# Block 0's tokens split a layer earlier, the first long unit begun inside the last output, and fetches, stores and splits of the second network reordered

## The chip, the cores and the metric

One core of one Trainium2 chip runs the whole program. The metric is the device time of one execution in microseconds; runs of this kernel are compared by their median. The profile comes from one execution of its own.

## The reference

Three layers follow each other: windowed attention (4 batches, 8 heads, 576 positions, head size 64, half of the heads with a dilated window), a gated network and a second network. x is the attention's output, 2304 tokens of 512 values.

```python
x = attention(q, k, v)                     # (2304, 512)
gate = 1.0 / (1.0 + np.exp(-(x @ w_gate)))     # 512 -> 1536
x = (gate * (x @ w_val)) @ w_out               # 1536 -> 512
h = x @ w_in                                   # 512 -> 2048
g = np.maximum(h, 0.0) + alpha * np.minimum(h, 0.0)
return g @ w_out2                              # 2048 -> 512
```

Everything is fp32 in and out. The kernel writes each operand as a high and a low fp16 half, scaled by powers of two, and makes each product from three matmuls (high x high, high x low, low x high).

## The kernel before

**Stages.** The program is one list of instructions for each engine, in the order in which the Python code issues them; nothing is reordered afterwards. A batch b has twelve steps m, in which `gv_mm` makes the gate's and the value's product into pairs of PSUM banks (three pairs in turn, `buffer`), ACT takes the sigmoid (L597), DVE multiplies (L602) and `gv_halves` makes the fp16 halves `gt` (L612 on ACT, the subtraction L170 on POOL or DVE). After that come four outputs d of the first network, each twelve groups `o1_mm(b, d, m)` of six matmuls of 288 columns (L636), evacuated by `o1_y` (L654), which stores y to DRAM (L656). I call the twelve steps layer 1 of the batch and the four outputs its layer 2. Between them `prepare` takes entries of a list of steps that make the second network's weights (w_in2 into `wi_dram`, w_out2 into `w2_dram`: L813 to L816 on POOL, L823 on ACT, L828 on DVE, stores L840 on SP). Batch 3 is the last; `last_output(d, m)` puts further work into its layer 2.

**The second network** works in token blocks: block 0 has 256 tokens, blocks 1 to 4 have 512. `y_load` fetches a block's y, `y_sums` makes differences on POOL, and ACT and DVE split them (`y_high` L925, `y_low` L929, or in steps, `y_steps` L914 and L915) into the tile `yh`. Block 0 is multiplied directly in four short units of two products each, which are issued at fixed points of outputs 2 and 3. Blocks 1 to 4 have four long units each, which use Strassen's scheme in Winograd's form: seven products P1 to P7 of twelve matmuls (L968, 256 columns) instead of eight. In a long unit the products pile up in banks: x takes P1, then P6, P5 and P3 on top; y takes P2; z takes P7, then P4. Since P1 alone is wanted too, ACT copies the bank x away (`copy`, L1023) ahead of each next product, and DVE adds the copies elsewhere (`plus`, L1026): c1 to P2, c4 and z for a22, c2 to z. `relu` (L1006) and `slopes` (L1014) make the activation, `g_high` (L1050) and `g_low` (L1054) its halves.

**Filling.** Behind each of a unit's seven products `spare()` takes items of the output product `out2_mm` (L1213) of the block before: three matmuls an item for block 0, six for the others, 56 items a block, spread evenly over the 28 slots of a block. `out2_done` evacuates a finished product on ACT or DVE (L1236, L1238) and issues its store (L1243).

**SP's queue** issues all DMAs in program order; an issue that waits holds up all behind it. `in2_fetch` (L761) brings the weights of a unit (two tiles of 896 KB; four tiles in a ring, two used, two ahead), `w2_fetch` (L1196) those of an output product (two of 512 KB; four places). Both are issued at the end of a unit, behind the stores that its items issued.

**Buffers.** The pool `yp` has 8 slots of 4 KB a partition, which all loads of words, quarters, halves and y share: a new tile waits until its slot's last reader, often a store, is done. The pool `tp` has two slots for each of the tags `sg` and `gf`.

The lines that set the place of block 0's splits, of the fetches, and of P1:

```python
            if d < 2 and m == 0:                       # last_output
                y_load(d)
            if d == 1 and m in (6, 8):
                y_high(0, m // 8)
                y_low(0, m // 8)
...
                unit(j, k, spare, n if n[0] < NJ else None)
                in2_release()
                while coming and ring_i:
                    in2_fetch(coming.popleft())
                w2_fetch_all()
```

## Time and profile before

| | us |
|---|---|
| runs shown | 857.73, 858.0, 858.41 |
| median | 858.0 |
| profiled execution | 857.94 |
| its span, first to last instruction | 856.1 |
| TensorE busy | 826.2 |
| VectorE busy | 601.8 |
| ScalarE busy | 438.4 |
| GpSimd busy | 263.8 |

The span is 1.84 us shorter than the profiled execution. Batch 3's layer 1 runs from 398 to 469.6 us, its layer 2 with the short units from 469.6 to 533.0, block 1 from 533.0 to about 589, blocks 2 to 4 and the last output product after that. A row of the time order gives the start, the duration, the engine, the line and the tiles, a count where alike instructions follow each other, and in brackets how long the engine had been idle and which instruction ended that. The printed end of a matmul group lies 0.16 us behind the start of the next where nothing waits.

### The profile page before, as it was taken

What the parts mean: (1) busy time and instruction counts of PE and PEld (TensorE: products, weight loads), DVE (VectorE), ACT (ScalarE), POOL (GpSimd) and SP (SyncE); (2) the same over time, 40 slices, a digit from 0 to 9 for tenths busy, and PEclk for the clock granted to TensorE, in tenths of its full rate; (3) what the DMA queues carried; (4) which work ended last, traced back from release to release, by engine and by line L of the source; (5) the groups of instructions that cost most, each with busy time, mean ns of one, the idle gap of its engine ahead of it and who ended that gap; (6) DMA issues with size and microseconds to landing.
All of it is one profiled execution on the core that took longest, in us unless ns stands there. A gap on an engine that the chain in (4) does not pass through costs nothing.

```text
span 856.1 us, 21080 instructions
## 1 busy us (share of the span) xinstructions
PE 826.2 (97%) x8994; PEld 686.5 (80%) x8994; DVE 601.8 (70%) x1046; ACT 438.4 (51%) x725; POOL 263.8 (31%) x253
## 2 busy tenths in 40 slices
PE   7699999999999999999999899998999999999998
PEld 4677787877877778777887678887888888888887
DVE  5889976776687677777859767588577577566641
ACT  4767664357435453444336556465555555454420
POOL 1324252234011011020238744343442245232220
PEclk9699999999999999999999999999999999999999
DMA  9954526334454252068667867955955655675372
GB/s 319 348 184 141 191 73 218 112 121 161 149 190 154 76 202 70 1 201 251 232 218 240 286 242 284 337 204 201 340 206 202 245 183 202 239 284 198 123 230 78
DMA packets 86621, 169.86 MB, mean 198 GB/s; under 512 B 5504, under 2 KB 57856, under 8 KB 86528
## 3 DMA queue, kind: packets, MB, share of 16 engines
q1 hardware_dynamic: 86528, 168.52, 56.8%
q8 instruction: 70, 1.15, 0.6%
q14 instruction: 23, 0.19, 0.1%
HBM read 138.72 MB, written 29.79 MB: 197 GB/s over the span
## 4 chain that ended last, share of the span: by engine, by line
PE 72%; DVE 12%; DMA 9%; ACT 3%; issue 2%; SPq 2%; POOL 0%; ACTq 0%; DVEq 0%
PE banks L584 20%; PE banks L1213 18%; PE banks L968 17%; PE banks L636 13%; DMA w_dram<-halves 2%; DVE plain L189 2%; DMA plain_dram<-plain 2%; DVE plain L185 2%; PE banks L317 2%; PE banks L431 1%; DVE halves L828 1%; DMA vc<-vk 1%; DMA q<-qbd 1%; DVE plain L181 1%; DVE gf L602 1%
## 5 line engine op out<-in xcount | busy, mean ns | idle before, releaser
L584 PE MATMUL banks<-xh,w_gv 128*128 128x288 f16 x2304 | 290.6, 287 | 0.5 <-ACT sg L597 0.3
L584 PEld LDWEIGHTS <-w_gv 128*128 128x128 f16 x2304 | 223.3, 98 | 58.4 <-issue 0.9
L968 PE MATMUL banks<-yh,w_i 128*128 128x256 f16 x1536 | 189.1, 274 | 10.0 <-ACT yh L925 2.5
L968 PEld LDWEIGHTS <-w_i 128*128 128x128 f16 x1536 | 150.6, 98 | 30.3 <-issue 8.0
L636 PE MATMUL banks<-gt,w_o 128*128 128x288 f16 x1152 | 144.5, 286 | 0.9 <-POOL gt L170 0.9
L636 PEld LDWEIGHTS <-w_o 128*128 128x128 f16 x1152 | 111.8, 98 | 28.9 <-issue 1.1
L1213 PEld LDWEIGHTS <-g_gv 128*128 128x128 f16 x780 | 76.3, 98 | 8.8
L1213 PE MATMUL banks<-w,g_gv 128*128 128x256 f16 x612 | 75.5, 273 | 0.0
L1006 ACT ACTIVATE neg<-banks 128x512 f32<-128x512 f32 x72 | 42.8, 594 | 56.9 <-DVE banks L1026 40.3
L1064 POOL TENSOR_TENSOR yh<-temp_y 128x512 f32<-128x512 f32 x16 | 26.5, 1659 | 125.6 <-DVE temp_y L1014 120.8
L166 POOL TENSOR_SCALAR sc<-sc 128x1 f32<-128x1 f32 x35 | 11.7, 334 | 173.0 <-DVE sc L162 172.9
L1213 PEld LDWEIGHTS <-g_g 128*128 128x128 f16 x564 | 55.2, 98 | 6.4
L602 DVE SCALAR_TENSOR_TENSOR gf<-banks,sg 128x576 f32<-128x576 f32 x48 | 36.0, 752 | 34.4 <-PE banks L584 25.5
L597 ACT ACTIVATE sg<-banks,sc 128x576 f32<-128x576 f32 x48 | 35.3, 734 | 39.9 <-PE banks L584 30.1
L196 ACT ACTIVATE junk<-plain 128x1024 bf16<-128x1024 f32 x32 | 33.8, 1057 | 36.0 <-DVE plain L200 18.8
L170 POOL TENSOR_TENSOR gt<-gf,gt 128x576 f16<-128x576 f32 x19 | 27.7, 1457 | 75.4 <-ACT gt L612 75.2
L612 ACT ACTIVATE gt<-gf 128x576 f16<-128x576 f32 x48 | 32.4, 677 | 33.3 <-DVE gf L602 29.4
L189 DVE SCALAR_TENSOR_TENSOR plain<-words,plain 128x512 uint32<-128x512 uint32 x64 | 47.7, 765 | 1.2
L1213 PE MATMUL banks<-w,g_g 128*128 128x256 f16 x396 | 48.3, 273 | 0.0
L1054 DVE SCALAR_TENSOR_TENSOR g_gv<-temp_w,sc,g_gv 128x256 f16<-128x256 f32 (+1 forms) x37 | 26.0, 711 | 28.4 <-ACT g_gv L1050 28.4
L1023 ACT ACTIVATE temp_y<-banks 128x512 f32<-128x512 f32 x32 | 19.0, 595 | 50.9 <-PE banks L968 50.7
L185 DVE SCALAR_TENSOR_TENSOR plain<-words,plain 128x512 uint32<-128x512 uint32 x64 | 43.8, 704 | 1.2
(178 smaller groups left out, 1212.3 us busy)
## 6 DMA issues: line engine op xcount, KB each, us to landing
w_i<-wi_dram SPq DMA_DIRECT2D x40, 896.0 KB, 6.3
w<-w_dram SPq DMA_DIRECT2D x52, 512.0 KB, 8.7
words<-w_out SPq DMA_DIRECT2D x28, 512.0 KB, 5.5
plain<-w_dram SPq DMA_DIRECT2D x18, 512.0 KB, 9.5
words<-w_in SPq DMA_DIRECT2D x16, 512.0 KB, 5.2
w_dram<-halves SPq DMA_DIRECT2D x28, 256.0 KB, 5.1
q<-qbd SPq DMA_DIRECT2D x6, 1152.0 KB, 7.6
words<-w_gate SPq DMA_DIRECT2D x12, 512.0 KB, 5.3
```

Source lines behind the costliest of these rows:

```text
L170: engine.tensor_tensor(out=lo, in0=src, in1=hi, op=ALU.subtract)
L185: nc.vector.scalar_tensor_tensor(out=d, in0=hi, scalar=0xC0000000, in1=d, op0=ALU.bitwise_and, op1=ALU.bitwise_or)
L189: nc.vector.scalar_tensor_tensor(out=d, in0=lo, scalar=29, in1=d, op0=ALU.logical_shift_right, op1=ALU.bitwise_or)
L196: nc.scalar.activation(junk[:, :src.shape[1]], src, AF.Square, accum_out=dst)
L584: nc.tensor.matmul(ps[:, h, :], lhsT=a, rhs=x_[:, H2 * h:H2 * h + H2], start=(kk == 0 and i == 0), stop=(kk == KD - 1 and i == 2),)
L597: nc.scalar.activation(halves(sg), ps, AF.Sigmoid, scale=sgx[b][:, m:m + 1])
L602: nc.vector.scalar_tensor_tensor(out=halves(gf), in0=ps, scalar=2.0 ** -15, in1=halves(sg), op0=ALU.mult, op1=ALU.mult)
L612: nc.scalar.activation(t[:, 0, :], gf, AF.Copy)
L636: nc.tensor.matmul(ps[:, h, :], lhsT=a, rhs=x_[:, H2 * h:H2 * h + H2], start=(m == 0 and z == 0), stop=(m == M1 - 1 and z == 2),)
L968: nc.tensor.matmul(o, lhsT=h, rhs=l, start=(new and v == 0 and q == 1), stop=(q == total_), skip_group_check=True,)
L1006: nc.scalar.activation(t[:, :2 * n], src[:, :2 * n], AF.Relu, scale=-1.0)
L1213: nc.tensor.matmul(ps[:, H4 * t:H4 * t + H4].rearrange("p (c f) -> p c f", c=2), lhsT=a, rhs=x_, start=(first and k == 0 and t == 0 and z ...
```

## The change

- Block 0's y is loaded at step m = 4 of batch 3's layer 1, into one yp slot; its differences are made at m = 6 and its splits at m = 7 and 8. `y_first` takes the first `xh` tile for them. The blocks' places in `yh` change sides (even and odd).
- `gv_halves` of the last step stands directly behind its multiply, with the subtraction on DVE, for every batch.
- `o1_y` of batch 3 uses the tag `gf` instead of `sg`.
- `unit_begin(1, 0)` (P1 and its copy) stands at step (3, 9) of layer 2. The copy goes from bank x into a bank y, and P2 is added on top of it; `plus c1` goes. y has two banks in turn (7 and 3), the output products have three instead of four.
- y of block 2 is loaded at (3, 4); its splits, and those of blocks 3 and 4, are spread over the slots of the block before.
- `in2_fetch` stands directly behind P4, `w2_fetch` behind the last item of a product, `out2_store_old` issues a store three items after its evacuation. The first w2 fetch moves from (3, 0) to (3, 8).
- Six items of block 1's own first output product are taken within block 1.

```diff
@@ o1_y
-        dst = tp.tile([P, S], F32, tag="sg", name="y")
+        dst = tp.tile([P, S], F32, tag="gf" if b == B - 1 else "sg", name="y")
@@ y_load, y_first, y_sums
+        if j == DIRECT:
+            t = yp.tile([P, 2, 2, n], F32, tag="y", name="y")
+            for d in range(2):
+                y[j, d] = t[:, d]
+                nc.sync.dma_start(out=t[:, d], in_=y_dram[:, d::2, t0:t0 + n])
+            return
...
+    def y_first():
+        n = blocks[DIRECT][1]
+        t = spans[0] = xp.tile([P, 4608], F16, tag="xh", name="yh")
+        z = 6 * n
+        yh[DIRECT] = [t[:, z * i:z * i + z].rearrange("p (d i t) -> p d i t", d=2, i=3) for i in range(2)]
+        temps["s2"] = t[:, 3584:].bitcast(F32)
...
         if j == DIRECT:
-            add(out=s[:, 0, :n], in0=t[:, 1, :n], in1=t[:, 0, :n], op=ALU.subtract)
+            s = y[j, d, "sums"] = temps["s2"][:, n * d:n * d + n].unsqueeze(1)
+            add(out=s[:, 0], in0=t[:, 1], in1=t[:, 0], op=ALU.subtract)
             return
@@ in2_bank
-            turn["h"] = (turn["h"] + (x_ != "y")) % 3
-            i = in2_order[3 if x_ == "y" else turn["h"]]
+            if x_ == "y1":
+                turn["y"] = 1 - turn.get("y", 0)
+                i = (in2_order[3], 3)[turn["y"]]
+            else:
+                turn["h"] = (turn["h"] + 1) % 3
+                i = in2_order[turn["h"]]
@@ unit_begin, unit
-        copy("c1", in2_mm(j, "x1", [(PART_A[1], PART_B[1])], True, w))
+        in2_mm(j, "x1", [(PART_A[1], PART_B[1])], True, w)
+        in2_bank("y1")
+        nc.scalar.activation(in2_banks["y1"], in2_banks["x1"], AF.Copy)
...
-        ps_y = mm(2, "y", True)
+        ps_y = mm(2, "y")
         rest(0)
-        plus(ps_y, "c1", ps_y)
...
-        ps_z = plus(ps_z, "c2", mm(4, "z"))
+        ps_z = mm(4, "z")
+        in2_release()
+        while coming and ring_i:
+            in2_fetch(coming.popleft())
+        plus(ps_z, "c2", ps_z)
@@ out2_mm, out2_done
-            turn["o"] = (turn.get("o", -1) + 1) % 4
+            turn["o"] = (turn.get("o", -1) + 1) % 3
...
             ring.append(w2q[i].popleft())
+            while ring and fetched:
+                w2_fetch(fetched.popleft())
...
-            nc.sync.dma_start(
+            stores.append([3 if len(items) > U else 0, lambda: nc.sync.dma_start(
...
+            out2_store_old()
@@ last_output
-            if d < 2 and m == 0:
-                y_load(d)
+            if (d, m) == (1, 0):
+                y_load(1)
...
-            if d == 1 and m in (6, 8):
-                y_high(0, m // 8)
-                y_low(0, m // 8)
...
+            if (d, m) == (3, 4):
+                y_load(2)
...
+            if (d, m) == (3, 8):
                 w2_ring(True)
                 w2_fetch(fetched.popleft())
+            if (d, m) == (3, 9):
+                short_order.clear()
+                turn.update(h=-1, y=1)
+                i = 2 * turn["m"]
+                in2_order.extend([6, 4, 5, 7] if i == 4 else [6, 5, 4, 7])
+                unit_begin(1, 0, [w_i[0], w_i[1]])
@@ batch loop
+                if m == M1 - 1:
+                    gv_halves(b, m, False)
...
+                if late and m == 4:
+                    y_first()
+                    y_load(DIRECT)
+                if late and m == 6:
+                    y_sums(DIRECT, 0)
+                    y_sums(DIRECT, 1)
+                if late and m in (7, 8):
+                    y_high(DIRECT, m - 7)
+                    y_low(DIRECT, m - 7)
-            gv_halves(b, M1 - 1, late)
@@ blocks 1 to 4
+            early = U - 2 if j == 1 else 0
+            items.extend((j, 1, k) for k in range(early))
...
-                if more and k in (1, 2):
-                    y_sums(j + 1, k - 1)
-                    background.extend([lambda: None] * 2 + y_steps(j + 1, k - 1))
+                    background.extend([lambda: None] * (7 * (U // 2)))
+                    first = 2 if j == 1 else 7
+                    background[first] = lambda j=j: y_sums(j + 1, 0)
+                    for d in range(2):
+                        for n, f in enumerate(y_steps(j + 1, d)):
+                            background[first + 2 + 9 * d + 3 * n] = f
+                    background[first + 9] = lambda j=j: y_sums(j + 1, 1)
```

The next rows show how this moves instructions. A name with a number is a tile, `banks_81` stands for all of PSUM, and line numbers of the changed kernel differ from those of the profile: its L946 is L929 before, L1131 is the new copy, L1044 is L1023, L1071 is L1050, L1222 is L1196, L1271 is L1243.

DVE between the multiplies of m = 8 and m = 9 in batch 3's layer 1 (halves and quarters are tiles of the w2 steps), before and then after:

```order
L602 SCALAR_TENSOR_TENSOR gf_6833<-banks_81,sg_6774 128x576
L828 SCALAR_TENSOR_TENSOR halves_6804<-quarter_6662,sc_78,halves_6804 128x512
L828 SCALAR_TENSOR_TENSOR halves_6804<-plain_6789,sc_78,halves_6804 128x512
L828 SCALAR_TENSOR_TENSOR halves_6835<-plain_6789,sc_78,halves_6835 128x512
L828 SCALAR_TENSOR_TENSOR halves_6835<-quarter_6659,sc_78,halves_6835 128x512
L828 SCALAR_TENSOR_TENSOR halves_6871<-plain_6790,sc_78,halves_6871 128x512
L602 SCALAR_TENSOR_TENSOR gf_6919<-banks_81,sg_6869 128x576
```

```order
L602 SCALAR_TENSOR_TENSOR gf_6843<-banks_81,sg_6784 128x576
L828 SCALAR_TENSOR_TENSOR halves_6814<-quarter_6666,sc_78,halves_6814 128x512
L828 SCALAR_TENSOR_TENSOR halves_6814<-plain_6799,sc_78,halves_6814 128x512
L946 SCALAR_TENSOR_TENSOR yh_6562<-y_6563,sc_78,yh_6562 128x512
L946 SCALAR_TENSOR_TENSOR yh_6562<-yh_6562,sc_78 128x256
L828 SCALAR_TENSOR_TENSOR halves_6845<-plain_6799,sc_78,halves_6845 128x512
L828 SCALAR_TENSOR_TENSOR halves_6845<-quarter_6663,sc_78,halves_6845 128x512
L828 SCALAR_TENSOR_TENSOR halves_6885<-plain_6800,sc_78,halves_6885 128x512
L602 SCALAR_TENSOR_TENSOR gf_6933<-banks_81,sg_6883 128x576
```

Two split instructions of block 0 now stand among the five w2 instructions; before, they stood behind all of them in layer 2.

ACT at the end of layer 2 (`y_7781` and `y_7795` are the last output, `neg` the activations, the copies come from banks), before and then after:

```order
L1050 ACTIVATE g_gv_7208<-temp_w_7206,sc_78 128x256 x3
L654 ACTIVATE y_7781<-banks_81,sc_78 128x576
L196 ACTIVATE junk_7783,sc_78<-y_7781 128x576
L1050 ACTIVATE g_gv_7208<-yh_7203,sc_78 128x256
L1050 ACTIVATE g_gv_7208<-temp_w_7206,sc_78 128x256
L1050 ACTIVATE g_gv_7208<-yh_7204,sc_78 128x256
L1050 ACTIVATE g_gv_7208<-temp_w_7206,sc_78 128x256
L1023 ACTIVATE yh_7205<-banks_81 128x512
L1023 ACTIVATE temp_y_7812<-banks_81 128x512
```

```order
L1071 ACTIVATE g_gv_7217<-temp_w_7215,sc_78 128x256 x3
L1131 ACTIVATE banks_81<-banks_81 128x512
L654 ACTIVATE y_7795<-banks_81,sc_78 128x576
L196 ACTIVATE junk_7797,sc_78<-y_7795 128x576
L1071 ACTIVATE g_gv_7217<-yh_7213,sc_78 128x256
L1071 ACTIVATE g_gv_7217<-temp_w_7215,sc_78 128x256
L1071 ACTIVATE g_gv_7217<-yh_6562,sc_78 128x256
L1071 ACTIVATE g_gv_7217<-temp_w_7215,sc_78 128x256
L1044 ACTIVATE temp_y_7826<-banks_81 128x512
```

The copy of P1 stood behind the output's evacuation and four `g_high`; now it stands ahead of them.

SP in block 1 (`out` is a store, `w_i` a unit's weights, `w_2` and `plain` places of w2), before and then after:

```order
L1243 DMA out<-temp_7808 128x256
L761 DMA w_i0_6622<-wi_dram_87 128x3584
L761 DMA w_i1_6623<-wi_dram_87 128x3584
L1196 DMA w_2_7813<-w2_dram_89 128x2048 x2
L1196 DMA plain_7589<-w2_dram_89 128x2048
L1196 DMA plain_7590<-w2_dram_89 128x2048
L1243 DMA out<-temp_y_7810 128x256
L1243 DMA out<-temp_7809 128x256
L761 DMA w_i2_6624<-wi_dram_87 128x3584
```

```order
L1222 DMA plain_7755<-w2_dram_89 128x2048
L1271 DMA out<-temp_7822 128x256
L761 DMA w_i0_6626<-wi_dram_87 128x3584
L761 DMA w_i1_6627<-wi_dram_87 128x3584
L1222 DMA w_2_7827<-w2_dram_89 128x2048 x2
L1271 DMA out<-temp_y_7824 128x256
L1222 DMA w_2_7827<-w2_dram_89 128x2048 x2
L1271 DMA out<-temp_7823 128x256
L761 DMA w_i2_6628<-wi_dram_87 128x3584
L761 DMA w_i3_6629<-wi_dram_87 128x3584
```

The w2 fetches stand between the stores, and a store stands three items behind the evacuation that it waits for.

## Rows read from the trace of the kernel before

**Rows 1.** The page's head and part 1: busy us, share, instructions.
```profile
span 856.1 us, 21080 instructions
...
PE 826.2 (97%) x8994; PEld 686.5 (80%) x8994; DVE 601.8 (70%) x1046; ACT 438.4 (51%) x725; POOL 263.8 (31%) x253
```

**Rows 2.** Busy us by stretch: length, PE, PEld, DVE, ACT, POOL, PEclk, DMA share, GB/s.
```profile
600.00:620.00 20.00, 20.00 (x186) 17.92 (x184) 11.20 (x19) 10.06 (x17) 9.41 (x9) 1.00 0.93 352
```

**Rows 3.** TensorE in order of time: start, us, line, tiles, count, idle before.
```profile
469.61 8.49 PE L636 MATMUL banks<-gt,w_o 128*128 128x288 f16 x68
478.97 10.21 PE L636 MATMUL banks<-gt,w_o 128*128 128x288 f16 x82 [0.87 <-POOL gt L170]
491.72 0.27 PE L968 MATMUL banks<-yh,w_i 128*128 128x256 f16 x1 [2.54 <-ACT yh L925]
492.56 0.49 PE L968 MATMUL banks<-yh,w_i 128*128 128x256 f16 x3 [0.57 <-DVE yh L929]
494.09 3.86 PE L968 MATMUL banks<-yh,w_i 128*128 128x256 f16 x20 [1.04 <-DVE yh L929]
...
499.99 2.78 PE L968 MATMUL banks<-yh,w_i 128*128 128x256 f16 x24
...
533.03 2.78 PE L968 MATMUL banks<-yh,w_i 128*128 128x256 f16 x24
536.97 2.78 PE L968 MATMUL banks<-yh,w_i 128*128 128x256 f16 x24 [1.15 <-ACT yh L1023]
...
574.53 1.47 PE L968 MATMUL banks<-yh,w_i 128*128 128x256 f16 x12 [1.03 <-ACT temp_y L1023]
...
577.29 1.47 PE L968 MATMUL banks<-yh,w_i 128*128 128x256 f16 x12 [0.63 <-DVE banks L1026]
...
580.16 1.48 PE L968 MATMUL banks<-yh,w_i 128*128 128x256 f16 x12 [0.75 <-DVE temp_y L1014]
...
589.17 0.83 PE L968 MATMUL banks<-yh,w_i 128*128 128x256 f16 x6 [0.97 <-DMA w_i<-wi_dram]
591.35 0.83 PE L968 MATMUL banks<-yh,w_i 128*128 128x256 f16 x6 [1.36 <-DMA w_i<-wi_dram]
```

**Rows 4.** Busy time by stretch at the second place, columns as before.
```profile
494.00:496.00 2.00, 1.91 (x10) 1.35 (x10) 0.52 (x2) 1.43 (x4) 1.12 (x2) 0.50 1.04 372
496.00:498.00 2.00, 2.00 (x14) 1.55 (x13) 0.00 (x0) 0.00 (x0) 2.00 (x4) 0.69 1.09 384
```

**Rows 5.** SP, ACT and POOL in order of time ahead of the first short unit.
```profile
474.94 3.84 SPq L870 DMA_DIRECT2D y<-y_dram  x2
...
484.75 1.99 ACT L823 ACTIVATE halves<-quarter,sc 128x512 f16<-128x512 f32 x3 [3.86 <-DMA w_dram<-halves]
...
489.59 0.84 POOL L902 TENSOR_TENSOR ys<-y 128x256 f32<-128x256 f32 x1 [4.20 <-DMA w_dram<-halves]
```

**Rows 6.** SP's queue at the end of block 1.
```profile
583.17 0.34 SPq L1243 DMA_DIRECT2D out<-temp  x1
583.61 0.87 SPq L761 DMA_DIRECT2D w_i<-wi_dram  x2
```

**Rows 7.** VectorE: line L828 (min/median/max ns), and the multiply of m = 10.
```profile
L828 DVE SCALAR_TENSOR_TENSOR halves<-quarter,sc,halves x16: 737/1085/1759, 450.5 to 489.1; 128x512 f16<-128x512 f32 x16
...
467.32 0.74 DVE L602 SCALAR_TENSOR_TENSOR gf<-banks,sg 128x576 f32<-128x576 f32 x1
```

**Rows 8.** Line L1023 and line L1026 (min/median/max ns), and the first copy of P1.
```profile
L1023 ACT ACTIVATE temp_y<-banks x32: 574/597/598, 538.5 to 807.8; 128x512 f32<-128x512 f32 x32
...
L1026 DVE TENSOR_TENSOR banks<-banks,temp_y x32: 684/692/700, 542.8 to 814.7; 128x512 f32<-128x512 f32 x32
...
536.34 0.57 ACT L1023 ACTIVATE yh<-banks 128x512 f32<-128x512 f32 x1
```

**Rows 9.** SP's first issue for long units; DMA of 520 to 556 us.
```profile
522.14 7.73 SPq L761 DMA_DIRECT2D w_i<-wi_dram  x4
...
DMA packets 3002, 11.96 MB, mean 332 GB/s; under 512 B 297, under 2 KB 297, under 8 KB 2999
```

More of the change, by code (lines that the diff above doesn't have):

```diff
@@ L1116, in unit @@
             unit_begin(j, k, w)
-        in2_banks["x"] = in2_banks.pop("x1")
+        in2_banks.update((x_, in2_banks.pop(x_ + "1")) for x_ in "xy")
         def mm(i, x_, new=False):
@@ L1242, in out2_done, with out2_store_old @@
             r0 = blocks[j][0] + P * nt * to[0]
-            nc.sync.dma_start(
+            stores.append([3 if len(items) > U else 0, lambda: nc.sync.dma_start(
                 out=out[r0:r0 + P * nt, H4 * to[1]:H4 * to[1] + H4].rearrange("(t p) c -> p t c", p=P),
                 in_=dst.rearrange("p (t c) -> p t c", c=H4),
-            )
+            )])
+            out2_store_old()
+    stores = deque()
+    items = deque()
+    def out2_store_old():
+        while stores and stores[0][0] <= 0:
+            stores.popleft()[1]()
     engines = (nc.gpsimd, nc.vector)
@@ L1417, in take @@
         def take(items):
+            for x_ in stores:
+                x_[0] -= 1
+            out2_store_old()
             j, i, k = items.popleft()
             out2_mm(j, i, k)
-            if k == U - 1 and j == NJ - 1:
-                w2_fetch_all()
         def w2_fetch_all():
@@ L1515, in attention_moe_kernel @@
         second_places()
-        short_order.clear()
-        turn["h"] = 0
-        i = 2 * turn["m"]
-        in2_order.extend([6, 4, 5, 7] if i == 4 else [4, 5, 6, 7])
         w2_ring(False)
-        items = deque((DIRECT, i, k) for i in ORDER for k in range(U))
+        items.extend((DIRECT, i, k) for i in ORDER for k in range(U))
         slots = [7 * (U // 2)]
@@ L1540, in spare @@
                 for _ in range(-(-len(items) // slots[0])):
-                    take(items)
+                    if (items[0][0], items[0][1], items[0][2] // 2) in g2:
+                        take(items)
             slots[0] -= 1
@@ L1551, in attention_moe_kernel @@
                 if more and k == 0:
-                    y_load(j + 1)
-                if more and k in (1, 2):
+                    if j > 1:
+                        y_load(j + 1)
                     assert not background
-                    y_sums(j + 1, k - 1)
-                    background.extend([lambda: None] * 2 + y_steps(j + 1, k - 1))
+                    background.extend([lambda: None] * (7 * (U // 2)))
[5 more added lines that the diff above has]
+                    background[first + 9] = lambda j=j: y_sums(j + 1, 1)
                 n = (j, k + 1) if k + 1 < U // 2 else (j + 1, 0)
                 unit(j, k, spare, n if n[0] < NJ else None)
-                in2_release()
-                while coming and ring_i:
-                    in2_fetch(coming.popleft())
-                w2_fetch_all()
             assert not items, len(items)
-            items.extend((j, i, k) for i in ORDER for k in range(U))
+            items.extend((j, i, k) for i in ORDER for k in range(early if i == 1 else 0, U))
         flush()
```

16 lines of the change are left out of this document (7 added, 9 removed).

## Prediction

> **What bounds the kernel now.** I read the page's head first, then busy time in stretches, then TensorE's own timeline with its waits, then the engines that it waits for. TensorE is busy 826.2 of 856.1 us [rows 1], and from 600 to 840 us, in twelve stretches of 20 us alike, it is busy throughout [rows 2]. The change neither adds nor removes a matmul, so it can only win back idle time of TensorE, and only between 460 and 600 us; what else it touches (the last halves of batches 1 and 2, the long units after 600) has no idle time behind it. The reader should see ten idle times there [rows 3], in five places:
>
> - 0.87 us in the last output of batch 3 (478.97), behind the low half of the last `gt` on POOL.
> - 2.54 + 0.57 + 1.04 = 4.15 us before the first short unit (491.72 to 494.09), behind the splits of block 0's tokens, L925 on ACT and L929 on DVE.
> - 1.15 us in the first long unit (536.97): P6 waits for ACT's copy of P1 out of the bank that P6 adds to.
> - 1.03 + 0.63 + 0.75 = 2.41 us in block 1 (574.53 to 580.16), behind ACT and DVE.
> - 0.97 + 1.36 = 2.33 us at the start of block 2 (589.17, 591.35), behind the weights `w_i`.
>
> They add up to 10.91 us. Behind the second place lies a further cost: the granted clock is 0.50 in 494 to 496 and 0.69 in 496 to 498 [rows 4], so half speed, the lower of its two levels, for part of that time; before, the engine had been almost idle for 5 us. In the row 494.09 twenty matmuls take 3.86 us; at the rate of the row 499.99 (24 in 2.78, of which 0.16 is the tail of the last) they would take 2.34. That is 1.5 us more. All in all 12.4 us can be had, and no more. The shorter stalls later (1.4 us at most) cost no clock.
>
> **Place 1, the last halves.** `gv_halves(11)` moves to right behind the last multiply and its subtraction from POOL to DVE. The multiply runs near 471.0 (3.7 us after its neighbour of m = 10 [rows 7]); with 0.7 us on ACT and 0.8 to 1.8 us on DVE the tile is ready by 474.5, and its matmuls start near 478. **-0.87.**
>
> **Place 2, block 0's splits.** Why are they late? `y_load(0)` sits in SP's queue until 478.8 (3.84 us for two issues), because its slots in the pool `yp` are still being stored from; all stores of halves queue behind it, ACT then waits 3.86 us for one of these stores, and POOL's subtraction 4.20 us for another [rows 5]. The change loads into one slot at m = 4 of the layer before, some 45 us earlier (seven steps of 48 matmuls before 469.6, 0.123 us each by the row 469.61), puts the sums into a spare part of the `xh` tile, and splits at m = 7 and 8. Its two sets are 4 ACT and 4 DVE instructions of 0.5 to 0.75 us, 2 POOL subtractions and 2 DMAs. The first set falls into a hole of DVE. The second stands between the multiplies of m = 8 and m = 9 in a stretch where DVE has no hole: 0.74 + 0.48 = 1.2 us alone, up to 2.9 us where POOL runs at the same time, since the 128x512 step L828 takes 737 ns at best and 1759 at worst [rows 7]. Everything behind it on DVE shifts, the multiply of m = 10 too. That ends at 468.06, and the first matmul of the last output, which reuses its bank, starts at 469.61: 1.55 us of room. So this costs 0 to 1.35 us; I take 0.3, since ACT also waits for DVE there and the shift is partly taken up. **-4.15 and -1.5 for the clock, +0.3.** The four yp slots no longer used make the w2 chain behind shorter, not longer.
>
> **Place 3, the first long unit.** P1 of unit (1, 0) is issued three steps ahead of the end of the last output: 18 matmuls, 2.2 us, stand behind it. ACT's copy moves ahead of the output's evacuation and of four `g_high`, so it no longer starts 2.0 us after P1's end (536.34 [rows 8]), and P6 finds its bank read. The short units that the early P1 could disturb are all issued; its banks (6, 7) were last used two units before. **-1.15.**
>
> **Place 4, block 1.** Three causes meet before: six split steps of block 2 in two bursts of consecutive slots (each an ACT and a DVE step over up to 1024 columns), the addition `plus c1` (692 ns [rows 8], once per unit), and groups of only six small matmuls between products. The change spreads the six steps over slots 4 to 19, drops `plus c1` (16 x 0.69 = 11 us of DVE over the whole kernel, off the path after 600), gives `y` two banks in turn, which removes the 0.75 us wait outright, and adds six full items of block 1's own P1 to the filling. A unit of DVE work is still near 12 us of a 13.8 us unit where two steps fall into it, so I keep a quarter: **-2.41, +0.6.**
>
> The new copy is PSUM to PSUM on ACT. No row shows ACT writing PSUM; the nearest are its copy to SBUF, 597 ns, and DVE writing PSUM, 692 ns [rows 8]. I take 0.6 us; it replaces a copy in the same place of ACT's queue, and between P1 and P2 lie P3, P4 and three groups (at least 4.6 us), so either end costs nothing. The Trainium skill ("ScalarE: Activation LUTs", Step-by-step: what each stage is for) says that ACT writes PSUM faster than SBUF; by it the copy would be under 597 ns, and the sum the same.
>
> **Place 5, the weights.** SP issues w_i for block 2 at 583.61, right behind an output store that stood at the queue's head until 583.17 [rows 6], while P4, which frees these tiles, had ended at 578.8 (577.29 + 1.47). The change defers each store by three items (2 to 3 us, about what DVE's evacuation took) and issues the fetch right behind P4, 4.8 us earlier, against 2.33 us of stall. **-2.33.** Out2 banks go from four to three: the bank that a product takes over was evacuated at least two products earlier, so this costs nothing.
>
> **The start of block 1, new.** The first w2 fetch moves back by eight steps behind two w_i pairs and y(2). With all TensorE work 5 us earlier, 11.8 MB (three w_i pairs of 1.84, y of 1.05, five w2 of 1.05) are asked for from about 516 us (the first pair went out at 522.14 [rows 9], less 5.0, less 0.9 for the two w2 issues that stood ahead of it), and the last of them are wanted at 552: the last output would end at 529.3 (533.03 less 5.0, and 1.3 later for the P1 put ahead), and 204 matmuls of 0.109 us and 0.35 us of small ones lie from there to P1 of unit (1, 2). Before, 520 to 556 moved 11.96 MB at a mean of 332 GB/s [rows 9]; at that pace they land at 551.6. So the order fits with 0.4 us to spare: 0 to 1 us; I take 0.3.
>
> **The sum.** The profiled execution took 857.94 us (span 856.1 and 1.84 around it), 0.06 under the median 858.0. 857.94 - 12.4 = 845.5; + 0.3 + 0.6 + 0.3 = **846.7 us**. With the low ends of the three costs it is 845.5, with their high ends (1.35, 2.4, 1.0) 850.3.
>
> **Rivals.**
> (a) *DMA is late at the start of block 1.* For it: 0.4 us of room; at a tenth less than the mean pace, 300 GB/s, the 11.8 MB take 39.3 us, the weights of unit (1, 2) come at 555.3, and about 3 us are lost: 849.5. Against it: shorter stretches reach 384 [rows 4]. The Trainium skill ("DMA: Bandwidth & Descriptors", Specifications) gives about 358 GB/s of HBM per core; as an estimate from that page the bytes would land at 549 and nothing would wait. Chance 0.14.
> (b) *The stalls behind DVE stay*: layer 1 loses its 1.35 us and block 1 keeps all of its 2.4 less the 0.75 of the second y bank: 845.5 + 1.35 + 1.65 + 0.3 = 848.8. Chance 0.16.
> (c) *The change doesn't do what it says:* block 0's splits are early, but POOL or ACT waits in its queue for the load, holds up the sigmoids of layer 1, and the 5.65 us of place 2 come back there: 852.4. Against it: the load is issued two steps (12 us) ahead of its use. Chance 0.05.
> (d) *Slower.* P2 now waits directly for ACT. Should ACT reach the copy late in every long unit, each of the 16 pays. It costs from 4.0 us of lag on (4.6 of cover less 0.6), and the kernel is slower than before from 4.0 + 12.4 / 16 = 4.8 us of lag; at 5.2 us it would be 845.5 + 16 x 1.2 = 864.7. Against it: the largest lag in the trace is 2.0 us, with six instructions ahead in the queue. Chance 0.03.
>
> **How the numbers follow.** Forecast 846.7 with 0.62. The range 845.3 to 850.5 takes in the forecast with its bounds and the scatter of the runs, (a) and (b), and leaves out (c), (d) and the cases in which more goes wrong. A measurement of this kernel can tell about 0.2% (1.7 us) from no change: faster 0.94, same 0.02, slower 0.04, the last two from (d) and from cases like (c) in which more comes back than place 2 gave.
>
> **What would show it.** Right: TensorE's granted clock is 1.00 throughout 480 to 500; the short units start behind the last output's first half without idle time; no wait of P6 for L1131; SP has no store at its head while w_i tiles are free; total idle time from 440 to 600 under 2 us. Wrong, and where: idle time before the first matmul of the last output (the DVE shift), at the first out2 product or at P1 of unit (1, 2) behind `w` or `w_i` (rival a), at P3 or P4 of block 1 behind ACT or DVE (rival b), at P2 behind L1131 (rival d).

## The result and the profile after

The changed kernel takes **844.31 us** (median of 4 runs, 844.09 to 846.11) where the kernel before takes 857.87 beside it (4 runs). The ratio of the means is 0.9848, with a 95% interval of 0.9831 to 0.9865. The profiled execution took 844.38 us with a span of 842.6; before it was 857.94 with 856.1. So 13.56 us are gone. The prediction said 846.7 us, 845.3 to 850.5, and that 12.4 us could be had at most: the direction and the places were right, but more came back than it held possible.

The head of the profile's page of after, and three of the seven stretches of 20 us from 460 to 600 (length, then TensorE, its weight loads, VectorE, ScalarE and GpSimd busy, granted clock, DMA share, GB/s):

```profile
span 842.6 us, 21055 instructions
...
PE 822.9 (98%) x8994; PEld 684.2 (81%) x8994; DVE 600.5 (71%) x1031; ACT 438.2 (52%) x725; POOL 271.4 (32%) x252
```

```profile
480.00:500.00 20.00, 20.00 (x174) 16.76 (x172) 15.69 (x19) 12.29 (x22) 13.11 (x13) 1.00 0.94 319
...
520.00:540.00 20.00, 19.90 (x191) 17.36 (x189) 13.08 (x32) 11.80 (x24) 7.20 (x12) 1.00 1.01 395
...
580.00:600.00 20.00, 20.00 (x185) 17.85 (x184) 13.84 (x26) 11.77 (x20) 6.78 (x5) 1.00 0.72 261
```

TensorE is busy throughout, but for 0.1 us in 520 to 540, and the granted clock is 1.00; the four stretches left out read the same in these two columns. None of the ten idle times of [rows 3] is left. Where three of the five places stood, TensorE's time order of after now reads (start, us, line, tiles, count; a bracket would give an idle time):

```profile
469.83 18.54 PE L636 MATMUL banks<-gt,w_o 128*128 128x288 f16 x150
488.20 2.78 PE L989 MATMUL banks<-yh,w_i 128*128 128x256 f16 x24
...
523.87 1.47 PE L989 MATMUL banks<-yh,w_i 128*128 128x256 f16 x12
525.17 2.37 PE L636 MATMUL banks<-gt,w_o 128*128 128x288 f16 x18
527.38 4.09 PE L989 MATMUL banks<-yh,w_i 128*128 128x256 f16 x36
...
532.97 1.40 PE L1239 MATMUL banks<-plain,g_gv 128*128 128x256 f16 x9
...
535.52 1.15 PE L1239 MATMUL banks<-plain,g_gv 128*128 128x256 f16 x9
```

The 150 matmuls of the last output run through (before, 68 and 82 with a pause between), and the short unit follows at once. P1 of the first long unit stands at 523.87, ahead of the last 18 matmuls of the output. The largest loss left is in the row 532.97: nine matmuls take 1.24 us to the next start where those of 535.52 take 0.98, so 0.26 us are lost; it is the first product that reads the fetched w2 weights. Two smaller losses show no bracket either, 0.08 us ahead of the group at 577.20 and 0.06 us ahead of the one at 581.84.

**A finer measure than the median.** The first instructions up to batch 3 differ little between the kernels, and yet the first matmul group of batch 3 starts anywhere from 396.38 to 399.78 us in the profiles of this study. Below I therefore compare the stretch from that start to the start of the last group of the program. Before (first two rows) and after (last two):

```profile
398.24 3.96 PE L584 MATMUL banks<-xh,w_gv 128*128 128x288 f16 x31
...
850.83 1.47 PE L1213 MATMUL banks<-w,g_y 128*128 128x256 f16 x12
```

```profile
398.47 3.72 PE L584 MATMUL banks<-xh,w_gv 128*128 128x288 f16 x29
...
837.29 1.47 PE L1239 MATMUL banks<-w,g_y 128*128 128x256 f16 x12
```

That is 850.83 - 398.24 = 452.59 us before and 837.29 - 398.47 = 438.82 us after: 13.77 us less. (The start is 0.23 us later in the profile of after, and the tail behind the last group is alike; 13.77 - 0.23 is 13.54, against 13.56 in the two profiled times.)

### The profile page after: what moved, and what is told of

It is laid out like the page before. It is cut to its first block, busy times and chain, and to the rows that moved or that the text cites. A ratio compares the mean times of both kernels' runs of the same rounds, so it can differ in the third digit from the quotient of the medians.

```text
span 842.6 us, 21055 instructions
## 1 busy us (share of the span) xinstructions
PE 822.9 (98%) x8994; PEld 684.2 (81%) x8994; DVE 600.5 (71%) x1031; ACT 438.2 (52%) x725; POOL 271.4 (32%) x252
## 3 DMA queue, kind: packets, MB, share of 16 engines
q8 instruction: 70, 1.15, 0.6%
## 4 chain that ended last, share of the span: by engine, by line
PE 88%; DVE 5%; DMA 4%; issue 1%; ACT 1%; SPq 1%; POOL 0%; ACTq 0%; POOLq 0%
PE banks L584 29%; PE banks L1239 20%; PE banks L989 19%; PE banks L636 16%; PE banks L317 2%; DMA q<-qbd 2%; PE banks L431 2%; DMA plain<-w_dram 1%; DVE plain L185 1%; DMA second<-qbd 1%; DVE plain L189 1%; DVE plain L181 1%; PE banks L446 0%; DVE xh L174 0%; DVE w_gv L174 0%
## 5 line engine op out<-in xcount | busy, mean ns | idle before, releaser
L989 PE MATMUL banks<-yh,w_i 128*128 128x256 f16 x1536 | 186.9, 273 | 0.0
L1239 PEld LDWEIGHTS <-g_gv 128*128 128x128 f16 x780 | 76.3, 98 | 9.1 <-issue 0.3
L170 POOL TENSOR_TENSOR gt<-gf,gt 128x576 f16<-128x576 f32 x18 | 26.0, 1444 | 73.8 <-ACT gt L612 73.6
L1075 DVE SCALAR_TENSOR_TENSOR g_gv<-temp_w,sc,g_gv 128x256 f16<-128x256 f32 (+1 forms) x37 | 27.7, 758 | 25.6 <-ACT g_gv L1071 25.5
L1089 POOL TENSOR_TENSOR temp_w<-temp_w,yh 128x512 f32<-128x512 f32 (+1 forms) x20 | 30.4, 1520 | 45.9 <-DVE g_g L1075 24.8
```

The lines of the kernel that those rows point to most:

```text
L989: nc.tensor.matmul(o, lhsT=h, rhs=l, start=(new and v == 0 and q == 1), stop=(q == total_), skip_group_check=True,)
L1089: add(out=a12, in0=a12, in1=s2, op=ALU.subtract)
L1239: nc.tensor.matmul(ps[:, H4 * t:H4 * t + H4].rearrange("p (c f) -> p c f", c=2), lhsT=a, rhs=x_, start=(first and k == 0 and t == 0 and z ...
```

## Experiments

All but one undo a single part in the changed kernel; e10 is the kernel before with one part alone. "Stretch" is the measure just described; "growth" is against after's 438.82, for e10 against before's 452.59.

| run | median us | ratio to before (95%) | stretch | growth |
|---|---|---|---|---|
| after | 844.31 | 0.9848 (0.9831 to 0.9865) | 438.82 | |
| e1 last halves on GpSimd | 846.13 | 0.9859 (0.9842 to 0.9877) | 442.05 | +3.23 |
| e2 block 0's splits late | 849.88 | 0.9901 (0.9885 to 0.9917) | 444.47 | +5.65 |
| e3 first long unit not begun early | 846.56 | 0.9869 (0.9845 to 0.9893) | 441.13 | +2.31 |
| e5 SP: w_i and stores as before | 858.25 | 0.9992 (0.9976 to 1.0008) | 453.40 | +14.58 |
| e6 SP: w_i, stores and w2 as before | 851.97 | 0.9944 (0.9920 to 0.9967) | 447.25 | +8.43 |
| e7 SP: stores alone as before | 845.37 | 0.9851 (0.9830 to 0.9872) | 439.00 | +0.18 |
| e8 first w2 fetch early | 844.98 | 0.9852 (0.9834 to 0.9870) | 440.27 | +1.45 |
| e9 splits in bursts | 845.81 | 0.9854 (0.9836 to 0.9873) | 439.70 | +0.88 |
| e10 before, SP's order alone | 858.14 | 0.9998 (0.9982 to 1.0013) | 451.98 | -0.61 |
| e11 first w2 fetch between | 844.50 | 0.9835 (0.9819 to 0.9851) | 438.57 | -0.25 |
| e12 addition of c1 kept | 845.54 | 0.9852 (0.9833 to 0.9871) | 439.97 | +1.15 |
| e13 no early items | 845.58 | 0.9850 (0.9835 to 0.9865) | 440.17 | +1.35 |

The medians can't order the runs that lie within some 1.5 us of each other. The stretch comes from one profile of each run, and no run repeats one, so its own scatter isn't measured. What speaks for it is that the start-to-start losses in the rows account for each growth within 0.1 us. e5's ten runs spread from 853.77 to 860.15 us, so its profile (859.06) stands for it less well than the others do for theirs.

### e1: the last halves on GpSimd

```diff
                 gv_multiply(b, m)
-                if m == M1 - 1:
+                if m == M1 - 1 and not late:
                     gv_halves(b, m, False)
...
+            if late:
+                gv_halves(b, M1 - 1, True)
             y_scale(b, 0, KD)
```

> The changed kernel with one part undone: the low half of batch 3's last gate tile is written by GpSimd again, at the old place behind the loop. Theory A (each stall costs its printed idle time plus the 0.16 us by which the modelled end of the group before it overhangs the next start): TensorE stands still once at the last output, printed idle near 0.87 us, and the time from batch 3's first matmul group to the last group of the program grows by 0.87 + 0.16 = 1.03 us. Rival B (the printed idle time is the whole cost): it grows by 0.87. Rival C (the multiply's earlier or later place on VectorE decides, not the engine): no idle time and no growth.

TensorE's rows of e1:

```profile
468.19 8.49 PE L636 MATMUL banks<-gt,w_o 128*128 128x288 f16 x68
478.31 3.96 PE L636 MATMUL banks<-gt,w_o 128*128 128x288 f16 x31 [1.64 <-POOL gt L170]
...
533.67 0.27 PE L1239 MATMUL banks<-plain,g_gv 128*128 128x256 f16 x1 [0.39 <-DMA plain<-w_dram]
534.91 1.03 PE L1239 MATMUL banks<-plain,g_gv 128*128 128x256 f16 x8 [0.97 <-DMA plain<-w_dram]
```

The old wait is back, and larger than expected (1.64 us, not 0.87), since GpSimd reaches its subtraction only at 476.55, behind four of 1.3 to 1.7 us. From the start at 468.19, 68 matmuls to the next would end at 476.52 (468.19 + 8.49 - 0.16); the next starts at 478.31. So the wait costs 1.79 us, 0.16 more than its bracket says: theory A's tail. The rest of the growth stands at the first w2 product, where e1 loses 1.67 us against after's 0.26: 1.79 + 1.67 - 0.26 = 3.20, measured 3.23.

### e2: block 0's splits late, with their new buffers

```diff
-                    y_load(DIRECT)
-                if late and m == 6:
-                    y_sums(DIRECT, 0)
-                    y_sums(DIRECT, 1)
-                if late and m in (7, 8):
-                    y_high(DIRECT, m - 7)
-                    y_low(DIRECT, m - 7)
...
+            if (d, m) == (0, 0):
+                y_load(DIRECT)
...
+            if d == 1 and m == 2:
+                y_sums(0, 0)
+                y_sums(0, 1)
+            if d == 1 and m in (6, 8):
+                y_high(0, m // 8)
+                y_low(0, m // 8)
```

> The changed kernel with block 0's load, sums and splits back at their old places in the last layer (load at (0,0), sums at (1,2), splits at (1,6) and (1,8)); its one-slot load and its new place for the sums are kept. Theory A (the place late in the layer is what made TensorE wait): three idle times near the old 4.15 us come back, plus 0.48 us of tails and 1.5 us at half clock: growth near 6.1 us. Rival B (the old stall came from slots of the pool that were still being stored from; one slot in place of four comes free earlier): the load goes out on time, idle under 1 us, no half clock, growth 0 to 1 us.

TensorE's rows of e2, and the granted clock in the stretches behind:

```profile
477.74 9.72 PE L636 MATMUL banks<-gt,w_o 128*128 128x288 f16 x78
490.56 0.27 PE L989 MATMUL banks<-yh,w_i 128*128 128x256 f16 x1 [3.10 <-ACT yh L942]
491.40 0.74 PE L989 MATMUL banks<-yh,w_i 128*128 128x256 f16 x3 [0.57 <-DVE yh L946]
492.46 3.52 PE L989 MATMUL banks<-yh,w_i 128*128 128x256 f16 x20 [0.32 <-DVE yh L946]
495.82 2.37 PE L636 MATMUL banks<-gt,w_o 128*128 128x288 f16 x18
```

```profile
492.00:494.00 2.00, 1.68 (x9) 1.08 (x8) 0.80 (x2) 1.32 (x3) 0.55 (x1) 0.50 1.01 357
494.00:496.00 2.00, 2.00 (x16) 1.58 (x15) 0.00 (x0) 0.00 (x0) 1.92 (x4) 0.77 1.08 382
```

Theory A holds: 3.99 us printed idle in three brackets, three tails (0.48), and half clock. Its price: 20 matmuls take 3.36 us to the next start and would take 2.18 at 0.109 us each, 1.18 us; the three ahead of them lose 0.25. Together 5.90; less the 0.26 that is not lost at the first w2 product here, 5.64, measured 5.65. Rival B falls. SP was through with the load at 474.84, 3.9 us sooner than in [rows 5] (3.3 us counted from the start of layer 2), and ScalarE still came late: between 465 and 500 us it waited 5.8 us for stores of halves, and GpSimd waited 5.5 us for this load. The place in the layer is the gain, not the one slot.

### e3: the first long unit not begun early

```diff
-                unit_begin(1, 0, [w_i[0], w_i[1]])
             if d > 1 and M1 * (d - 2) + m in (1, 4, 6, 9, 11, 14, 16, 19):
```

> The changed kernel, but the first long unit's P1 is issued at its old place behind the last output. P2 now adds into the bank that ScalarE's copy writes, so it stands right behind the copy, where before one group (1.47 us) lay between. Theory A (the copy starts 2.0 us behind P1's end as in the kernel before, and then takes 0.6 us): TensorE stands still 2.6 us in front of P2, growth near 2.7 us. Rival B (the earlier splits and halves leave ScalarE ahead, the copy starts at once): idle 0.7 us, growth under 1 us.

TensorE and ScalarE of e3:

```profile
525.77 1.47 PE L989 MATMUL banks<-yh,w_i 128*128 128x256 f16 x12
529.64 4.09 PE L989 MATMUL banks<-yh,w_i 128*128 128x256 f16 x36 [2.40 <-ACT banks L1131]
```

```profile
525.97 0.74 ACT L654 ACTIVATE y<-banks,sc 128x576 f32<-128x576 f32 x1 [1.17 <-PE banks L636]
...
529.02 0.57 ACT L1131 ACTIVATE banks<-banks 128x512 f32<-128x512 f32 x1
```

Theory A holds. The copy stands behind the output's evacuation and (in the rows left out) four `g_high`, as in the kernel before, and starts 1.9 us behind P1. Because P2 adds into the copied bank, the stall is 2.40 us where before it was 1.15 [rows 3]. So the new data path by itself is worse here; the earlier P1 is what pays for it. Growth: 2.40 + 0.16 - 0.26 = 2.30, measured 2.31. The clock stayed at 1.00 through this pause.

### e5, e6, e7: SP's order

e5 takes w_i and the stores back, e6 also the w2 fetches, e7 the stores alone. e6:

```diff
         ps_z = mm(4, "z")
-        in2_release()
-        while coming and ring_i:
-            in2_fetch(coming.popleft())
...
             ring.append(w2q[i].popleft())
-            while ring and fetched:
-                w2_fetch(fetched.popleft())
...
-            stores.append([3 if len(items) > U else 0, lambda: nc.sync.dma_start(
+            stores.append([0, lambda: nc.sync.dma_start(
...
                 unit(j, k, spare, n if n[0] < NJ else None)
+                in2_release()
+                while coming and ring_i:
+                    in2_fetch(coming.popleft())
+                w2_fetch_all()
```

> The changed kernel with SP's order as before: w_i released and fetched at the end of each unit, output stores issued at once. Theory A (a store at the queue's head keeps the fetch of w_i back): the two idle times at the start of block 2 come back, 2.33 us printed, and with 0.16 us each the growth is 2.65 us; SP stands at a store of the output while w_i tiles are free. Rival B (everything runs 5 us earlier and SP is less behind, or the filling with early items shifts the stores): less than 0.5 us.

> As in the run before (stores at once, w_i fetched at the end of each unit), and the w2 fetches too are issued at the end of a unit behind w_i, not right behind each product. The run before lost 14.6 us from batch 3's first group on, and its SP stood 195 us at w2 fetches whose buffer a running product still read, with the w_i fetches behind them. Theory A (those w2 fetches at SP's head are the cause): with them behind w_i the loss falls to the old block-2 stalls, 2.3 to 2.8 us. Rival B (the later w_i fetch itself is the cause, since the early filling makes TensorE reach the weights sooner): the loss stays above 8 us.

> The changed kernel; only the output stores are issued at once again (w_i and w2 fetched early as changed). Theory A (a store whose tile VectorE has not finished keeps the fetches behind it back, as at 583.17 in the kernel before): idle time behind w_i in block 2, 1 to 2.5 us. Rival B (with the fetch behind P4 the store stands behind the fetch in the queue and holds up nothing that is needed soon): under 0.3 us.

e5 was a miss by 12 us: it lost all that the change had won. Its seven brackets with tails come to 10.5 us, and matmuls at the lower clock behind two of the pauses cost 4.2 us more. What SP waited for between 540 and 700 us in e5 (us in total, times, longest):

```profile
SPq L1219 <- PE banks L1236: 92.7, 15, 15.9
SPq L761 <- PE banks L989: 18.1, 7, 8.1
```

L1219 is the w2 fetch. In e5 it is queued right behind each product, as in the changed kernel, but w_i is queued at the end of the unit, behind it. The wait alone doesn't make the loss: in after SP stands 76.3 us at the same fetches in this window. What counts is what is queued behind it. SP's rows of e5 and, below, TensorE's:

```profile
557.35 0.80 SPq L1219 DMA_DIRECT2D w<-w_dram  x2
558.20 1.02 SPq L761 DMA_DIRECT2D w_i<-wi_dram  x2
...
577.59 0.90 SPq L761 DMA_DIRECT2D w_i<-wi_dram  x2
```

```profile
568.30 0.83 PE L989 MATMUL banks<-yh,w_i 128*128 128x256 f16 x6 [1.82 <-DMA w_i<-wi_dram]
...
583.54 1.27 PE L989 MATMUL banks<-yh,w_i 128*128 128x256 f16 x6 [1.96 <-DMA w_i<-wi_dram]
585.82 1.46 PE L989 MATMUL banks<-yh,w_i 128*128 128x256 f16 x6 [1.00 <-DMA w_i<-wi_dram]
```

The first of these pairs leaves right behind a w2 fetch, at 558.20, 159.65 us behind batch 3's first group; in e6 and in after it leaves 157.2 us behind theirs, and no wait for it follows. The second leaves at 577.59; in after it leaves at 570.10, 7.5 us sooner. With the w2 fetch behind w_i (e6) 6.2 us of the loss go away, so that one order was worth that much beside the late w_i. Most of them were lost at 568.30 and, further on, at 660.72 to 666.78 and 682.08. At the start of block 2 e6 loses as much as e5 (6.2 and 6.1 us), and its growth is still 8.43 us, not the 2.65 of theory A. e6 fits rival B in size. Its stalls are behind w_i too, at 580.71 (1.74 us), 584.24 (2.70) and 658.50 (1.25), one of 0.78 us behind w2, and the clock falls again: 0.50 in 584 to 586 and 0.69 in 586 to 588. Four brackets with tails are 7.1 us, and the rows 584.24 and 585.49 take 1.5 us longer than at full clock. What differs from the kernel before is that TensorE comes sooner: in e6 SP issues the pair at 575.61, behind a store that stood at the queue's head until 575.18, and TensorE wants it at 579.0, 3.4 us on; before, the pair left at 583.61 [rows 6] and TensorE wanted it near 588.2, 4.6 us on. This is read from the rows; no run isolates it.

e7 is small (0.18 us, all of it at the first w2 product). With the fetch ahead of them in the queue, the stores hold up nothing: rival B. So of SP's order the early place of w_i, right behind P4, is what counts, and once w_i is late, its place relative to the w2 fetches. The deferral of stores is worth nothing that these rows show while w_i is fetched early; no run defers them with w_i late.

### e10: SP's order alone, in the kernel before

The diff is e6's turned round, put into the kernel before.

> The kernel before with SP's order alone changed: w_i fetched right behind P4, each w2 fetch right behind its product, output stores three items late. Theory A (each part is worth the idle time that it removes): the two idle times at the start of block 2 go, 2.33 + 2 x 0.16 = 2.65 us, and the time from batch 3's first group to the last falls from 452.59 to 449.9 us. Rival B (the 8.4 us that the same part cost when it was undone in the changed kernel belong to it alone, wherever it stands): a fall of more than 5 us, which would need idle time that the trace of before does not have. Rival C (VectorE, late in block 1, keeps the place): no change.

The stretch falls by 0.61 us, not by 2.65. TensorE's rows of e10 from 550 us on:

```profile
557.76 0.83 PE L968 MATMUL banks<-yh,w_i 128*128 128x256 f16 x6 [1.27 <-DMA w_i<-wi_dram]
...
589.33 1.47 PE L968 MATMUL banks<-yh,w_i 128*128 128x256 f16 x12 [0.62 <-ACT temp_y L1023]
...
594.21 1.48 PE L968 MATMUL banks<-yh,w_i 128*128 128x256 f16 x12 [0.75 <-DVE temp_y L1014]
```

The two waits for w_i at the start of block 2 are gone as promised, and of block 1's own waits the first (1.03 us) shows no bracket any more. Three others stand in their place: one for w_i at 557.76, whose pair left at 546.74 between w2 fetches at 544.73 and 551.28 (before, the pair stood ahead of them), and two behind ScalarE and VectorE in block 2; that the old waits had given these engines time there is my reading, which no run isolates. Of block 1's own waits 0.64 and 0.75 us stay, at 575.84 and 578.72. The same part is worth 0.6 us alone, of the order of the scatter of a median, and 8.4 us in company (e6). All three theories miss; C is nearest.

### e8 and e11: where the first w2 fetch stands

```diff
-            if (d, m) == (3, 8):
+            if (d, m) == (3, 0):
                 w2_ring(True)
                 w2_fetch(fetched.popleft())
```

e11 has (3, 5) in that place.

> The changed kernel; the first w2 fetch is issued at the start of the last output again, eight steps sooner, ahead of two pairs of w_i and of y(2). Theory A (the fetch at 522.97 lands when its first product is due, 533: 0.26 us lost in the changed kernel, 1.4 and 0.4 us in two of its variants): nothing is lost there and the time falls by 0.26 us, to 438.56 us from batch 3's first group to the last group. Rival B (what goes out ahead of w_i delays w_i by the same bytes, 1.05 MB or 3 us): idle time at P3 or P4 of the first long units behind w_i, 0.5 us or more.

> The changed kernel; the first w2 fetch is issued at (3,5) of the last output, behind the first pair of w_i and y(2) and ahead of the second pair. Theory A (the first pair is what P1 of the first long unit waits for when w2 goes first, 1.5 us in that run, and the second pair has room): no idle time behind w2 nor behind w_i, time from batch 3's first group to the last 438.56 us, 0.26 less than in the changed kernel. Rival B (the second pair is late now): idle time at P1 of unit (1, 1), near 540 us, above 0.3 us.

In e8 the loss moves and grows: P1 of the first long unit waits 1.50 us for w_i at 525.30. Rival B, with the wait earlier than I had said. In e11 there is none. SP and TensorE of e11:

```profile
516.11 0.86 SPq L761 DMA_DIRECT2D w_i<-wi_dram  x2
...
518.68 1.42 SPq L1222 DMA_DIRECT2D plain<-w_dram  x2
522.59 1.63 SPq L761 DMA_DIRECT2D w_i<-wi_dram  x2
```

```profile
534.28 1.15 PE L1239 MATMUL banks<-plain,g_gv 128*128 128x256 f16 x9
535.27 1.47 PE L989 MATMUL banks<-yh,w_i 128*128 128x256 f16 x12
```

Nine matmuls take 0.99 us to the next start, and no bracket stands between batch 3 and the end. The stretch is 438.57 us against 438.56 expected. By the stretch e11 is 0.25 us better than after, the 0.26 us that it doesn't lose at the first w2 product; by the medians the two are the same.

### e9, e12, e13: the parts of block 1

```diff
-                    background.extend([lambda: None] * (7 * (U // 2)))
...
+                if more and k in (1, 2):
+                    assert not background
+                    y_sums(j + 1, k - 1)
+                    background.extend([lambda: None] * 2 + y_steps(j + 1, k - 1))
```

```diff
         in2_bank("y1")
-        nc.scalar.activation(in2_banks["y1"], in2_banks["x1"], AF.Copy)
+        copy("c1", in2_banks["x1"])
...
         rest(0)
+        plus(ps_y, "c1", ps_y)
```

```diff
-            early = U - 2 if j == 1 else 0
+            early = 0
```

> The changed kernel; the six split steps of the next block's tokens again stand in two bursts of consecutive slots. Theory A (the bursts made TensorE wait in block 1, 1.03 and 0.63 us printed): 1.66 + 0.32 = 2.0 us more. Rival B (the dropped addition, the second y bank and the early items alone leave enough room on VectorE): less than 0.3 us; VectorE busy 9 us or more in some stretch of 10 us, without a wait of TensorE.

> The changed kernel; ScalarE copies P1 to SBUF as before, P2 starts in its own bank, and VectorE adds the copy (0.69 us, once per unit, 16 times). The two banks of y stay. Theory A (0.7 us more of VectorE in a unit of near 12 us is what block 1 lacked): TensorE waits behind VectorE in block 1, 0.5 to 1.5 us in all. Rival B (the spread splits leave room for it): no idle time in block 1, less than 0.2 us; after 600 us nothing either way. Rival C (P2 no longer waits for the copy, but P7 and P3 wait for the addition): idle time at P3 or P2 in many units, above 2 us.

> The changed kernel without the six items of block 1's own P1 that fill its slots, so that the groups between its products are again of six small matmuls. Theory A (short fillings let TensorE run into the evacuations of VectorE and ScalarE): idle time in block 1 behind VectorE or ScalarE, 0.5 us or more. Rival B (the other three edits of block 1 suffice): less than 0.2 us. Rival C (with TensorE earlier at the weights and less room for the fetch of w_i, the wait comes at the start of block 2 instead): idle time behind w_i near 580 us.

TensorE's brackets in block 1 of e9, e12 and e13, in this order:

```profile
571.04 1.47 PE L989 MATMUL banks<-yh,w_i 128*128 128x256 f16 x12 [0.46 <-DVE banks L1047]
```

```profile
582.40 1.47 PE L989 MATMUL banks<-yh,w_i 128*128 128x256 f16 x12 [1.05 <-ACT temp_y L1058]
```

```profile
575.02 1.47 PE L989 MATMUL banks<-yh,w_i 128*128 128x256 f16 x12 [0.73 <-ACT temp_y L1044]
579.67 1.47 PE L989 MATMUL banks<-yh,w_i 128*128 128x256 f16 x12 [0.55 <-ACT temp_y L1044]
```

Each of the three edits does something: without the spread splits 0.62 us come back in block 1 (0.46 + 0.16; another 0.40 is printed at the first w2 product), without the dropped addition 1.21, without the early items 1.60. Theory A holds for e13, and in sign for e9, at a third of its size. In e12 the size is theory A's, but TensorE waits for ScalarE's copy (L1058, at 581.77), and it is ScalarE that had stood 1.04 us for VectorE until 581.14. Together the three are 3.4 us, more than the 2.41 + 0.48 that block 1 lost before, so in part they pay for the same room. No run undoes the second bank of y by itself, nor the tag of `o1_y`, the earlier load of block 2's y or the three output banks; what these are worth alone is not known.

## Why the prediction was wrong

**The step that failed is the ceiling**: "They add up to 10.91 us" and, with 1.5 us for the clock, "All in all 12.4 us can be had, and no more." A bracket counts from the printed end of the group before, and that end lies 0.16 us behind the point at which the next group could start. The prediction took this tail into account for the 24 matmuls of one row, and not for the ten idle times. So what ten waits cost is 10.91 + 10 x 0.16 = 12.51 us, and with 1.52 us for the clock 14.03. The starts in the trace of before say the same: at 478.97, for one, 68 matmuls at 0.1225 us should have taken 8.33 us and took 9.36, so 1.03 us where 0.87 is printed. e11, which has no printed wait, shows the floor: 452.59 - 438.57 = 14.02 us. Single waits agree: 2.40 printed is 2.56 over that floor in e3 (441.13 - 438.57), 0.27 is 0.43 in e7, 0.73 + 0.55 is 1.60 in e13, 1.50 is 1.70 in e8.

**The costs were the second error**, smaller: 1.2 us were kept back (0.3 in layer 1, 0.6 in block 1, 0.3 for the weights); 0.26 came at the weights, nothing in layer 1, and 0.14 in block 1, which a loss of 0.09 in the kernel before (680.44 to 681.84) nearly offsets. Redone with both, 857.94 - 14.03 + 0.26 is 844.17, and with a start that was 0.23 later in this profile 844.40; it took 844.38. The low end of the range, 845.3, had been set 0.2 us below what the ceiling leaves, so the range fell with it; with the tails it would have begun at 843.7.

Point by point:

- **Place 1** held: no idle time, but not with the room that was claimed. The tile was said to be ready by 474.5. In fact ACT waited 3.68 us for a store in front of its half, VectorE came at 476.32 and ended at 477.9, when its matmuls were due near 478.1. VectorE and ScalarE of after:

```profile
476.32 1.59 DVE L170 TENSOR_TENSOR gt<-gf,gt 128x576 f16<-128x576 f32 x1 [3.29 <-ACT gt L612]
```

```profile
474.39 1.33 ACT L823 ACTIVATE halves<-quarter,sc 128x512 f16<-128x512 f32 x2 [3.68 <-DMA w_dram<-halves]
475.63 0.67 ACT L612 ACTIVATE gt<-gf 128x576 f16<-128x576 f32 x1
```

- **Place 2** held, and e2 gives its worth, 5.9 us with the clock. The cost on VectorE in layer 1 was 0 of the 0 to 1.35 us: the second set took 2.2 us there (456.81 to 458.97), and still the multiply of m = 10 ended at 469.36, ahead of the output's start at 469.83.

```profile
456.81 0.74 DVE L946 SCALAR_TENSOR_TENSOR yh<-y,sc,yh 128x512 f16<-128x512 f32 x1
457.47 1.50 DVE L946 SCALAR_TENSOR_TENSOR yh<-yh,sc 128x256 f16<-128x256 f32 x1
...
468.62 0.74 DVE L602 SCALAR_TENSOR_TENSOR gf<-banks,sg 128x576 f32<-128x576 f32 x1
```

- **Place 3** held; e3 shows that the early P1 is worth 2.56 us in the new data path, twice the 1.31 (1.15 printed) of the old one.
- **Place 4**: 0.14 us was left of the 0.6 us kept. VectorE has no gap in 548 to 552 of after (4.00 of 4.00 us busy), yet TensorE does not wait there.
- **Place 5** held for after, but the price of 2.33 us belongs to the waits of the trace of before, not to the edit (e6, e10), and the deferral of stores, one of its two means, did nothing that e7 shows.
- **Rival (a)** was the right place: the largest loss left is there, 0.26 us, and up to 1.67 in e1. Its pace was too low: in 516 to 541 DMA moved 379 GB/s, against the 332 of [rows 9]. The page "DMA: Bandwidth & Descriptors" of the Trainium skill (Specifications) gives about 358 GB/s of HBM per core, and the measurement, of a program on one core, passes that too. **Rivals (b) to (d)** did not come. The new copy takes 582 ns from PSUM to PSUM, against 597 to SBUF in the same trace, which agrees in sign with what the page "ScalarE: Activation LUTs" of the Trainium skill (Step-by-step) says; nothing hangs on 15 ns:

```profile
L1131 ACT ACTIVATE banks<-banks x16: 580/582/593, 525.4 to 778.5; 128x512 f32<-128x512 f32 x16
```

```profile
L1044 ACT ACTIVATE temp_y<-banks x32: 572/597/597, 530.6 to 794.3; 128x512 f32<-128x512 f32 x32
```

## What to carry to other kernels

To price a wait, take start to start: the start of the waiting group less the point at which the group before would have let it start, not the printed idle time; with ten waits the difference decided whether the forecast held. The worth of an edit is not the idle time that it removes in the trace at hand: the one reordering of SP's queue was worth 0.6 us alone and 8.4 us beside the others, and in e10 three new waits stand where old ones were taken away. Undone one by one, the parts of the table (e1, e2, e3, e6, e9, e12, e13) cost 23.0 us, where together they brought 13.77: the parts can't be priced by adding such runs. Where one fetch of a queue is moved, look at what now stands behind it: in e5 a w2 fetch that waited for a buffer still in use held up the w_i fetch behind it.

## What was not expected of the hardware

- The length of a pause alone did not tell whether the granted clock fell. It stayed at 1.00 through 2.40 us (e3, 526 to 534) and through 1.82 us (e5, 566 to 570). It fell behind 1.96 us in e5: the row 583.54 already takes 1.27 us for six matmuls where the row 568.30 takes 0.83, and the clock is 0.50 in 584 to 590. It also fell at a pause of 3.10 us with short ones behind it (e2, 0.87 in 490 to 492, 0.50 in 492 to 494), at pauses of 1.74 and 2.70 us with 0.8 us of matmuls between (e6, 0.50 in 584 to 586), and at 1.67 and 1.18 us with 0.8 us between (e5, 0.57 in 662 to 664). The fall came inside the pause in e6 (583.5 to 584.0, ahead of the row 584.24) and in the second case of e5 (662.25 to 662.5), and shortly behind the restart in the first case of e5 and in e2; what it cost stands in the matmuls behind it, 1.4 to 1.5 us, and 2.8 us in the first case of e5.
- DMA moved more than the means of before suggest (352 GB/s over 20 us, 332 over 36): 411 and 417 GB/s in 520 to 524 and 524 to 528 of after, 379 over 25 us.
- Batch 3 starts anywhere from 396.82 to 399.78 us in after and its variants, whose instructions up to there are the same. Those 3 us are more than most parts of this change are worth; where they arise was not examined.
